# Two FFN channel blocks at a time: pair tiles in PSUM and instructions of 1024 columns

## The chip, the core and the metric

The kernel runs on one core of a Trainium2 chip. The metric is the device time of one execution in microseconds, the median of several runs. All runs told of here gave correct results. A ratio is the mean time of one kernel's fast runs over the mean of the other's fast runs of the same rounds, so it is not quite the ratio of the medians that stand beside it.

Engines are named as the profile names them: PE is TensorE, PEld its weight loads, DVE VectorE, ACT ScalarE, POOL GpSimd, SP the queue that issues DMAs.

## The reference, cut to what matters

An attention block with 32 inducing points is followed by a SwiGLU feed-forward block (FFN). B is 4, N 12416, C 128, and d_ff 1536, which is twelve channel blocks of 128.

```python
def mab(q, kv):                       # attention, softmax over the keys
    s = scale * (q @ kv.transpose(0, 2, 1))
    a = np.exp(s - s.max(-1, keepdims=True)); a /= a.sum(-1, keepdims=True) + 1e-09
    return a @ kv
x = mab(x, mab(I, x)).reshape(B * S, D)
xn = x / np.sqrt(np.mean(x * x, -1, keepdims=True) + 1e-06) * rms_g
g = xn @ w_gate
out = (g * (1 / (1 + np.exp(-g))) * (xn @ w_val)) @ w_out
```

## The kernel before

The FFN is done in 100 units of up to 512 tokens, each with twelve blocks. A *slot* is one block: a gate product, its silu on ACT, a value product, and the multiply of the two on DVE. The result `t` then has to be multiplied by `w_out` and summed over the blocks in `acc`. This *projection product* is not done at once. It goes into a queue, and each slot takes one or two products out of the queue between its gate and its value product. So PE has something to do while ACT and DVE work on the slot.

```python
for j in range(NJ):                                   # in ffn(), NJ = 12
    g = ps_gv.tile([P, 512], F32, name="gv", tag="gv")          # pool of 4 banks
    nc.tensor.matmul(g[:, 0:T], sg[:, ts(j, P)], a[:, 0:T], start=True, stop=True)
    sl = silp.tile([P, 512], F32, name="silu")
    nc.scalar.activation(sl[:, 0:T], g[:, 0:T], AF.Silu)
    products(j)                                       # takes products from the queue
    v = ps_gv.tile([P, 512], F32, name="gv", tag="gv")
    nc.tensor.matmul(v[:, 0:T], sv[:, ts(j, P)], a[:, 0:T], start=True, stop=True)
    t = up.tile([P, 512], F32, name="u")
    nc.vector.tensor_tensor(out=t[:, 0:T], in0=sl[:, 0:T], in1=v[:, 0:T], op=ALU.mult)
    steps(j)                                          # attention and seam work planned here
    if (b, u, j) in ready:
        soon(1, lambda j=j, t=t: three(j, t))         # a split: hi, lo, d
    else:
        plain.append(lambda j=j, t=t: project(wo[:, j, :], t[:, 0:T]))
```

A projection product is either *plain* (fp32) or *split*. In the split form `t` is taken apart into `hi`, `lo` and `d` by two ACT copies and two POOL subtractions, and three products on operands of type fp32r take the place of the fp32 one. In the trace an fp32r product of 512 columns takes PE 0.23 us and a plain fp32 one 0.86 us, so a split saves PE about 0.17 us. A loop plans the splits as far as POOL has time, and notes in `ready` from which slot on PE may use the operands. The queue is emptied like this:

```python
count = max(len(plain) - 1, 0) + sum(at <= now for at, _ in kara)   # kara: splits
... # held back for a few slots before an exponential
for _ in range(min(count, 2 if count > spare else 1)):   # spare is RESERVE = 3 mostly
    ...
# planning, per block:  (SLOT, SPLIT = 1.25, 2.75 us)
begin = max(free, now + 2.2 * SLOT)
...
free = begin + SPLIT
ready[b, u, j] = int((free + 0.3) / SLOT) + 1
```

Every four units there is a *seam*, where the attention weights of the next section are normed and prepared. Its last step, in slot 9 of a unit, is this:

```python
nc.vector.transpose(out=aT[rows, 0:w], in_=sc[b][rows, cols2[s]])
if b or s:
    nc.scalar.copy(out=hi[rows, 0:w], in_=aT[rows, 0:w])      # on ACT
...
engine.tensor_tensor(out=lo[...], in0=aT[...], in1=hi[...], op=ALU.subtract)   # on POOL
```

## Time and profile before

| | before |
|---|---|
| median of 3 runs | 1710.03 us (1707.98 to 1710.25) |
| span of the profiled run | 1708.1 us, mean granted PE clock 0.995 |
| silu, multiply | 1200 each, 0.60 and 0.68 us at 512 columns |
| plain products, splits | 817 and 383 |

The lines behind this are shown in the prediction. They are read in this order: the busy table says that only PE is full; the chain says that PE sets the end; the timeline of PE, start to start, says what a product costs.

Each stretch from one gate product to the next holds a known list of matmuls. The start-to-start steps of undisturbed stretches give each its time: 0.231 us for an fp32r product of 512 columns, 0.865 us for a plain fp32 one, less at 480 and 256 columns, and values found in the same way for the attention's products. What a stretch takes beyond the sum of its steps is called its *wait* here. From 90 us on, the waits of the kernel before sum to 61.9 us.

### The profile page before, as it was taken

Reading aid. Unit: us, or ns where it says so; the run is one execution under the profiler, and the core shown is the slowest. Engines: PE = TensorE matmul, PEld = TensorE weight load, DVE = VectorE, ACT = ScalarE, POOL = GpSimd, SP = SyncE. Lnnn points to the kernel's source line nnn. Section 1 sums busy time; section 2 is a strip of 40 time slices with the busy share of each in tenths; the row PEclk is TensorE's granted clock in tenths of the full one; section 3 lists DMA queues with packets and bytes.
Section 4 is the critical chain, followed back from the end, with each engine's and each line's share of the span. In section 5 each row is a group of like instructions: output and inputs, shape, how many; then the busy total and the mean of one; then the engine's idle time right before and its main releaser. Section 6 shows DMA issues by size and latency. Waiting matters only on the chain.

```text
span 1708.1 us, 23142 instructions
## 1 busy us (share of the span) xinstructions
PE 1668.0 (98%) x6781; PEld 1036.0 (61%) x6781; DVE 1145.0 (67%) x1914; ACT 1224.3 (72%) x2179; POOL 1146.2 (67%) x919
## 2 busy tenths in 40 slices
PE   8799999999999999999999999999999999999998
PEld 7445565655566666665556666566556666666666
DVE  4767775676667776667666777566756666666665
ACT  4446777676787777766678777767677887788786
POOL 1217775677587777677658777577657878887774
PEclk9899999999999999999999999999999999999999
DMA  6344533533354332433335314153211111111111
GB/s 261 74 68 75 70 80 60 121 75 69 56 78 68 49 65 51 105 75 88 65 57 90 57 34 87 28 131 79 54 31 33 35 36 33 33 36 36 33 37 24
DMA packets 389358, 112.64 MB, mean 66 GB/s; under 512 B 365136, under 2 KB 369776, under 8 KB 386672
## 3 DMA queue, kind: packets, MB, share of 16 engines
q1 hardware_dynamic: 388944, 111.02, 33.1%
q8 instruction: 54, 0.88, 0.2%
q14 instruction: 72, 0.59, 0.1%
q10 hardware_dynamic: 288, 0.15, 0.0%
HBM read 53.95 MB, written 27.00 MB: 47 GB/s over the span
## 4 chain that ended last, share of the span: by engine, by line
PE 87%; ACT 4%; DVE 3%; issue 2%; POOL 2%; DMA 1%; SPq 1%; ACTq 0%; DVEq 0%; POOLq 0%
PE acc L560 40%; PE gv L610 16%; PE gv L615 14%; PE u L578 5%; PE u L576 5%; PE mm L310 2%; DVE u L617 1%; PE mm L485 1%; ACT silu L612 1%; PE mm L368 1%; DVE aT L507 1%; PE gv L301 1%; ACT hi L510 1%; ACT hs L602 1%; POOL xn L603 1%
## 5 line engine op out<-in xcount | busy, mean ns | idle before, releaser
L617 DVE TENSOR_TENSOR u<-silu,gv 128x512 f32<-128x512 f32 (+2 forms) x1200 | 790.7, 666 | 512.1 <-PE gv L615 262.6
L612 ACT ACTIVATE silu<-gv 128x512 f32<-128x512 f32 (+2 forms) x1200 | 696.6, 584 | 370.1 <-PE gv L610 326.2
L560 PE MATMUL acc<-u,wo 128*128 128x512 f32 (+2 forms) x1634 | 811.5, 581 | 4.4 <-DVE u L617 3.1
L615 PE MATMUL gv<-a,sv 128*128 128x512 f32 (+2 forms) x1200 | 774.1, 645 | 3.7 <-DVE u L617 3.5
L598 POOL TENSOR_TENSOR xn<-u,xn 128x512 fp32r<-128x512 f32 (+2 forms) x383 | 482.2, 1259 | 356.0 <-ACT xn L597 295.1
L610 PE MATMUL gv<-a,sg 128*128 128x512 f32 (+2 forms) x1200 | 490.2, 409 | 12.8 <-ACT silu L612 8.5
L603 POOL TENSOR_TENSOR xn<-hs,u 128x512 fp32r<-128x512 f32 (+2 forms) x383 | 481.9, 1258 | 23.2 <-ACT hs L602 22.0
L610 PEld LDWEIGHTS gv<-a,sg 128*128 128x128 f32 x1200 | 227.2, 189 | 259.3 <-ACT silu L612 127.5
L560 PEld LDWEIGHTS acc<-u,wo 128*128 128x128 f32 x1634 | 305.1, 189 | 84.6 <-issue 18.2
L615 PEld LDWEIGHTS gv<-a,sv 128*128 128x128 f32 x1200 | 227.2, 189 | 204.1 <-issue 141.9
L597 ACT ACTIVATE xn<-u 128x512 fp32r<-128x512 f32 (+2 forms) x383 | 237.0, 619 | 15.6 <-DVE u L617 13.9
L602 ACT ACTIVATE hs<-xn 128x512 f32<-128x512 f32 (+2 forms) x383 | 235.7, 615 | 4.5 <-POOL xn L603 3.1
L560 PE MATMUL acc<-xn,xn 128*128 128x512 f32 (+2 forms) x383 | 149.7, 391 | 6.1 <-POOL xn L603 6.1
L578 PE MATMUL u<-xn,xn 128*128 128x512 f32 (+2 forms) x383 | 149.2, 390 | 0.0
L576 PE MATMUL u<-xn,xn 128*128 128x512 f32 (+2 forms) x383 | 147.8, 386 | 0.0
L499 POOL TENSOR_TENSOR rs<-ms,mhalf 128x16 f32<-128x16 f32 (+2 forms) x28 | 75.5, 2696 | 35.3 <-DVE ms L497 34.9
L560 PEld LDWEIGHTS acc<-xn,xn 128*128 128x128 f32 x383 | 71.8, 187 | 25.7 <-POOL xn L603 10.5
L578 PEld LDWEIGHTS u<-xn,xn 128*128 128x128 f32 x383 | 71.9, 188 | 15.6
L576 PEld LDWEIGHTS u<-xn,xn 128*128 128x128 f32 x383 | 72.1, 188 | 14.0
L569 DVE STREAM_TRANSPOSE o<-o 128x512 f32<-128x512 f32 (+2 forms) x97 | 67.7, 698 | 3.4
L568 DVE TENSOR_TENSOR o<-acc,o 128x512 f32<-128x512 f32 (+2 forms) x97 | 64.9, 669 | 0.0
L581 ACT ACTIVATE o<-u 128x512 f32<-128x512 f32 (+2 forms) x97 | 56.4, 581 | 0.2
(153 smaller groups left out, 735.0 us busy)
## 6 DMA issues: line engine op xcount, KB each, us to landing
out_dram<-o SPq DMA_DIRECT2D x320, 64.0 KB, 2.0
xT<-in_x_dram SPq DMA_DIRECT2D x60, 256.0 KB, 4.9
xn<-in_x_dram SPq DMA_DIRECT2D x60, 256.0 KB, 4.7
a<-hi SPq DMA_DIRECT2D x160, 64.0 KB, 2.0
a<-lo SPq DMA_DIRECT2D x158, 64.0 KB, 2.0
w<-w SPq DMA_DIRECT2D x22, 256.0 KB, 3.2
xn<-in_x_dram SPq DMA_DIRECT2D x5, 1024.0 KB, 10.9
out_dram<-o SPq DMA_DIRECT2D x64, 60.0 KB, 2.0
```

The source lines that it names most:

```text
L499: nc.gpsimd.tensor_tensor(out=rs, in0=ms, in1=mhalf[rows, 0:n], op=ALU.pow)
L560: nc.tensor.matmul(acc[:, 0:T], lhsT, rhs, start=st["left"] == NJ, stop=st["left"] == 1)
L576: nc.tensor.matmul(ups[:, 0:T], w[:, i, :], hi, start=st["k"] == nk, stop=False)
L578: nc.tensor.matmul(ups[:, 0:T], w[:, NK + i, :], lo, start=False, stop=not st["k"])
L597: nc.scalar.activation(hi, v, AF.Copy, scale=1.0 - 2.0 ** -13)
L598: nc.gpsimd.tensor_tensor(out=lo, in0=v, in1=hi.bitcast(F32), op=ALU.subtract)
L602: nc.scalar.activation(hs[:, 0:T], hi.bitcast(F32), AF.Copy, scale=1.0 + 2.0 ** -12)
L603: nc.gpsimd.tensor_tensor(out=d, in0=hs[:, 0:T], in1=v, op=ALU.subtract)
L610: nc.tensor.matmul(g[:, 0:T], sg[:, ts(j, P)], a[:, 0:T], start=True, stop=True)
L612: nc.scalar.activation(sl[:, 0:T], g[:, 0:T], AF.Silu)
L615: nc.tensor.matmul(v[:, 0:T], sv[:, ts(j, P)], a[:, 0:T], start=True, stop=True)
L617: nc.vector.tensor_tensor(out=t[:, 0:T], in0=sl[:, 0:T], in1=v[:, 0:T], op=ALU.mult)
```

## The change

The aim is fewer, larger elementwise instructions, so that fixed costs are paid half as often, and room for more splits. Blocks are taken in pairs; gate and value have one two-bank PSUM tile each; splits are made in pairs as well. To make room in SBUF, rows of x arrive in half tiles through one buffer, and the seam's product moves from POOL to DVE.

```diff
-    KJ = [j for j in range(NJ - 2) if j % 5 in (0, 2)] + [NJ - 3]
+    KJ = [j for j in range(NJ) if j % 4 < 2]
-    SLOT, SPLIT, RESERVE = 1.25, 2.75, 3
+    SLOT, UPPER, SPLIT, RESERVE = 1.25, 2.6, 4.85, 3
 ... (cut: pools, x rows in half tiles)
-        for j in range(NJ):
-            g = ps_gv.tile([P, 512], F32, name="gv", tag="gv")
 ... (cut: the loop shown above)
+        for j in range(0, NJ, 2):
+            pair = range(2)
+            g, v = (ps_gv.tile([P, 2, 512], F32, name=name) for name in ("g", "v"))   # bufs=1
+            for i in pair:
+                nc.tensor.matmul(g[:, i, 0:T], sg[:, ts(j + i, P)], a[:, 0:T], start=True, stop=True)
+            sl = silp.tile([P, 2, 512], F32, name="silu")
+            nc.scalar.activation(sl[:, :, 0:T], g[:, :, 0:T], AF.Silu)
+            products(j)
+            for i in pair:
+                nc.tensor.matmul(v[:, i, 0:T], sv[:, ts(j + i, P)], a[:, 0:T], start=True, stop=True)
 ... (cut: a slot of 1024 columns for u)
+            nc.vector.tensor_tensor(out=slot[0][:, :, 0:T], in0=sl[:, :, 0:T], in1=v[:, :, 0:T], op=ALU.mult)
+            steps(j)
+            products(j + 1)
+            steps(j + 1)
 ... (cut: three() on 1024 columns, with two sets of hi, lo, d in place of four)
-            nc.vector.transpose(out=z[...], in_=ps[rows, 0:w])
-            engine.tensor_tensor(out=z[...], in0=z[...], in1=weights(b, s), op=ALU.mult)
+            nc.vector.tensor_tensor(out=flat, in0=ps[rows, 0:w], in1=st["eT"][rows, 0:w], op=ALU.mult)
+            nc.vector.transpose(out=flat, in_=flat)
 ... (cut)
+            upper = now + 2 * SLOT + UPPER
+            begin = max(free, upper)
+            if begin > upper + SLOT:
+                continue
```

## The prediction

> **What bounds the kernel now.** I first read the busy table of the page, to see which engine has no room.
>
> ```profile
> span 1708.1 us, 23142 instructions
> PE 1668.0 (98%) x6781; PEld 1036.0 (61%) x6781; DVE 1145.0 (67%) x1914; ACT 1224.3 (72%) x2179; POOL 1146.2 (67%) x919
> PE 87%; ACT 4%; DVE 3%; issue 2%; POOL 2%; DMA 1%; SPq 1%; ACTq 0%; DVEq 0%; POOLq 0%
> ```
>
> The third line is the chain that ended last, by engine. TensorE is 98% busy and 87% of the chain; the other engines have 28 to 33% of the span free. Busy PE time is partly modelled, so I looked at how fast slots follow each other in the timeline of PE. A slot is one FFN channel block: gate product (L610), projection work, value product (L615).
>
> ```profile
> 805.30 0.39 PE L610 MATMUL gv<-a,sg 128*128 128x512 f32 x1
> 805.53 1.02 PE L560 MATMUL acc<-u,wo 128*128 128x512 f32 x2
> 805.99 0.79 PE L615 MATMUL gv<-a,sv 128*128 128x512 f32 x1
> 806.62 0.40 PE L610 MATMUL gv<-a,sg 128*128 128x512 f32 x1
> ...
> 813.32 0.39 PE L576 MATMUL u<-xn,xn 128*128 128x512 f32 x1
> 813.56 0.40 PE L578 MATMUL u<-xn,xn 128*128 128x512 f32 x1
> 813.79 0.39 PE L560 MATMUL acc<-xn,xn 128*128 128x512 f32 x1
> 814.02 0.40 PE L615 MATMUL gv<-a,sv 128*128 128x512 f32 x1
> 814.25 0.39 PE L610 MATMUL gv<-a,sg 128*128 128x512 f32 x1
> 814.49 0.59 PE L560 MATMUL acc<-u,wo 128*128 128x512 f32 x1
> ```
>
> Start to start, one fp32r product takes 0.23 us (813.56 to 813.79). A slot with the plain fp32 projection takes 806.62 - 805.30 = 1.32 us, so that projection costs 1.32 - 2 x 0.23 = 0.86 us. A slot whose projection is split into three fp32r products takes 5 x 0.233 = 1.165 us (813.32 to 814.49 is five such steps, 1.17). Over the whole trace the medians are 1.33 us (531 plain slots) and 1.16 us (251 split slots). So **one split saves PE about 0.167 us**. That is the only thing in this kernel that shortens PE's work, and the number of splits is limited by GpSimd and ScalarE, which make the three operands.
>
> I then subtracted these step times from all 1,199 intervals between gate products. About 40 us is left as waiting between 60 us, when the FFN starts, and 1700 us; some 10 us of it lies before 90 us, and some 10 us around the exponentials of the attention. So the rest of the run is PE work back to back.
>
> **The Trainium skill.** "FP8 and Floating Point Precision", section "TensorE Precision Notes", says that true fp32 takes four passes through the array. The trace agrees: 0.86 us is close to four times 0.23 us, and slightly less, so the split wins a little under one pass. "PSUM — Partial Sum Buffer", section "The four PSUM rules", says that one matmul's output fits in one bank; a 1024-column pair still needs two matmuls, so pairing removes no PE instruction. "Perfetto Trace Analysis", section "Optimizing Scalar/DVE Operations", says that each ScalarE and VectorE operation has a per-instruction overhead, that larger operations help an engine that is saturated, and that breaking them up can help where the engine isn't saturated but causes bubbles elsewhere. By the busy table the second case is nearer. The overhead shows in the groups kept apart by form:
>
> ```profile
> L617 DVE TENSOR_TENSOR u<-silu,gv 128x512 f32<-128x512 f32 x960 | 648.4, 682 | 409.0 <-PE gv L615 208.7 <-ACT hs L602 71.1 <-ACT xn L597 66.0
> L612 ACT ACTIVATE silu<-gv 128x512 f32<-128x512 f32 x960 | 570.6, 597 | 309.7 <-PE gv L610 269.2 <-DVE u L617 9.0 <-DVE xn L539 1.9
> L598 POOL TENSOR_TENSOR xn<-u,xn 128x512 fp32r<-128x512 f32 x318 | 410.2, 1290 | 272.5 <-ACT xn L597 219.8 <-PE gv L610 50.0 <-PE u L576 0.2
> L617 DVE TENSOR_TENSOR u<-silu,gv 128x256 f32<-128x256 f32 x48 | 19.4, 416 | 14.4 <-PE gv L610 5.5 <-PE gv L615 3.4 <-ACT silu L612 3.2
> L603 POOL TENSOR_TENSOR xn<-hs,u 128x256 fp32r<-128x256 f32 x15 | 11.0, 736 | 0.6 <-ACT hs L602 0.6
> L612 ACT ACTIVATE silu<-gv 128x256 f32<-128x256 f32 x48 | 18.2, 379 | 9.2 <-PE gv L610 9.0
> ```
>
> A straight line through 256 and 512 columns gives for 1024: DVE 682 + 2 x 266 = 1214 ns (fixed part 150), silu 597 + 2 x 218 = 1033 ns (161), POOL 1290 + 2 x 554 = 2398 ns (182). The two split copies on ACT (414 at 256, 627 to 631 at 512) become about 1055 ns. These are estimates from the trace.
>
> **The change part by part.**
>
> *Elementwise work.* 1200 silus become 600, about 604 us in place of 697; 1200 multiplies become 600, about 709 us in place of 791. Both engines run beside PE, so these 93 and 82 us are not on the path that sets the end. What they buy is room for splits.
>
> *More splits.* The planning loop at the end of the kernel is plain arithmetic. Worked through for the kernel before it gives 383, which is the x383 of the trace (318 of 512 columns, 50 of 480, 15 of 256). With the new constants (candidates are the pairs starting at 0, 4 and 8; 4.85 us of GpSimd a pair, which fits 2 x 2.398) it accepts 235 of 300 pairs: 9 fall at the ends, 21 at the marks for exponentials, 35 because GpSimd is planned busy. That is 470 splits (394, 64, 12), 87 more. Worth on PE: (76 x 0.167) + (14 x 0.157) - (3 x 0.08) = **14.6 us less**. PE matmul instructions rise by about 87 net, as a split has three and a plain product two.
>
> *Load after it.* POOL: 470 halves cost about 1105 us in place of 964, less 32 us for the product moved to DVE: some 1255 us. ACT: 1224 - 93 + 15 = about 1146. DVE: 1145 - 82 + 19 + 5 (product of the norm and extra partial sums) = about 1087. No engine reaches PE's total.
>
> *Buffers.* Before, gate and value products share four banks in turn, so a gate product waits for the silu of two slots earlier. After, gate and value have one two-bank tile each, and the next pair waits for the previous one. Take a pair with one plain and one split product, 4 x 0.2325 + 0.865 + 0.70 = 2.49 us on PE. Gate products start at 0 and 0.23, the second ends 0.40 later, silu runs from 0.66 to 1.69, and the bank pair is wanted at 2.49: slack 0.8 (0.6 in a pair with two splits, 2.33 us). The value products end near 1.9, the multiply runs to about 3.15, and they are wanted again at about 3.75: slack 0.6. In the kernel before the same sums give 1.3 to 1.5 us for both. A regular pair therefore does not stall, but PE has less reserve against a burst: the output step on DVE (683 + 712 ns), a seam transpose that ACT must wait for, or a hi or hs copy of 1.05 us. The trace before shows such a case near 820 us: DVE transposes aT until 819.77, ACT copies it until 820.40, silus follow, PE waits. With pairs I expect roughly 0.4 us more at each of the 24 seams and a few us elsewhere.
>
> *Moved work.* The norm's product goes from POOL to DVE (28 of 0.68 us), shortening that chain by 0.6 us each. Rows of x arrive in half tiles, five slots (6 us) ahead; landing takes 4.7 us at the median for twice the size, so I expect little waiting.
>
> *Sum.* -14.6 us of PE work, +5 to +9 us of waits: about -8 us, **1702 us**.
>
> **The rivals.** First: the single two-bank buffers stall PE in every pair. For it: slack falls from 1.4 to 0.6 us. Against it: it stays positive in the worst regular pair. A stall of 0.1 us in each of 600 pairs would be 60 us, and the time 1755. Second: nothing more stalls, or fewer handoffs even shorten the waits of 40 us by 5 to 10 us; the time is then 1686 to 1695. For it: half as many waits on ACT and DVE, and POOL loses a step in the seams; against it: the waits at start and exponentials do not depend on pairing. Third: GpSimd becomes the bound; a pair takes 4.80 us of POOL and two pairs take 4.98 us on PE, so a late operand stalls PE in order. The kernel before already has 7 such waits, 6.1 us. The planner keeps about 1 us in hand; if that fails at a tenth of 235 pairs by 1 us, it costs 23 us and the time is about 1720. Fourth: the x half tiles come late at some of the 36 uses; 0.5 us each is 18 us.
>
> **Range and chances.** Faster than 1676 needs over twice the gain of the splits, and waits cannot give back 20 us of 40: 0.04. Slower than 1744 needs a stall of the first rival's kind: 0.07. The rest, 0.89, is within 2%. Eight in ten: 1684 to 1727.
>
> **What would show it.** Right if the splits count 470, plain slots fall from 817 to 730, one 1024-column multiply takes near 1.21 us and the POOL steps near 2.4 us, the mean of a steady unit falls a little, and waits of PE on silu and multiply grow by less than 10 us. Wrong if pairs repeat slower than 2.49 us without POOL as releaser (first rival), or PE waits on L603's successor (third) or on x loads (fourth) by tens of us.

## The result

| | before | after |
|---|---|---|
| median | 1709.4 us (1707.98 to 1710.25, 4 runs) | 1786.39 us (1785.24 to 1787.85, 4 runs) |
| span, mean granted PE clock | 1708.1 us, 0.995 | 1785.1 us, 0.989 |
| plain products, splits | 817, 383 | 730, 470 |
| waits after 90 us, by the count above | 61.9 us | 152.4 us |

The ratio is 1.0452 (95% interval 1.0434 to 1.047): the changed kernel is 4.5% slower. These are the busy table and the chain of the changed kernel:

```profile
span 1785.1 us, 21312 instructions
PE 1684.9 (94%) x6868; PEld 1049.0 (59%) x6868; DVE 1122.3 (63%) x1360; ACT 1167.7 (65%) x1282; POOL 1259.7 (71%) x596
PE 73%; DVE 12%; issue 5%; ACT 4%; POOL 2%; DMA 2%; SPq 1%; DVEq 0%; ACTq 0%; POOLq 0%
```

PE is still the busiest engine, but its share of the chain has fallen from 87 to 73%, and that of DVE has risen from 3 to 12%. No engine is full. The groups kept apart by form show that each instruction costs what was foreseen (1214, 1033 and 2398 ns):

```profile
L645 ACT ACTIVATE silu<-g 128x1024 f32<-128x1024 f32 x480 | 491.8, 1025 | 328.6 <-PE g L643 258.0 <-DVE u L653 48.8 <-DVE xn L653 12.9
L653 DVE TENSOR_TENSOR u<-silu,v 128x1024 f32<-128x1024 f32 x386 | 469.9, 1217 | 388.1 <-PE v L648 318.2 <-ACT silu L645 59.3 <-POOL xn L629 7.3
...
L629 POOL TENSOR_TENSOR xn<-xn,u 128x1024 fp32r<-128x1024 f32 x158 | 379.2, 2400 | 9.3 <-ACT xn L628 7.0 <-DMA out_dram<-o 1.1
```

A regular pair runs as foreseen too. In the timeline of the changed kernel these are three gate pairs in a row, with one split and one plain product in each of the two pairs:

```profile
1502.96 0.63 PE L643 MATMUL g<-a,sg 128*128 128x512 f32 x2
...
1505.04 1.02 PE L643 MATMUL g<-a,sg 128*128 128x512 f32 x2
...
1507.92 0.39 PE L643 MATMUL g<-a,sg 128*128 128x512 f32 x1
```

Two pairs take 1507.92 - 1502.96 = 4.96 us, 2.48 us each; 2.49 had been worked out. (The middle start lies in the shadow of a plain product, as the records place the product after an fp32 pair some 0.4 us early.) Over the whole trace, 480 pairs hold two products; with that shadow taken out, half of them wait 0.02 us or less, but 85 wait over 0.25 us. So the time is lost in particular places. The list of waits has, of the kernel before (who waited for whom: us in total, times, longest):

```profile
ACT hi L510 <- DVE aT L507: 40.2, 27, 4.4
...
PEld gv L615 <- DVE u L617: 11.4, 27, 3.4
...
PE gv L610 <- ACT silu L612: 8.5, 16, 1.0
...
PE gv L615 <- DVE u L617: 3.5, 4, 3.0
```

and of the changed kernel:

```profile
PEld v L648 <- DVE u L653: 114.6, 268, 3.3
...
ACT hi L526 <- DVE aT L523: 47.7, 25, 4.6
...
PE g L643 <- ACT silu L645: 39.3, 36, 3.9
...
PE v L648 <- DVE u L653: 25.0, 41, 2.8
```

PE now waits for the silu (39.3 us, 8.5 before) and for the multiply (28.5 us, of which 3.5 us stand in a further line, where it was 3.5 before). ACT's own wait for the seam's transpose aT is hardly longer than before (40 and 48 us); in the kernel before it hardly reached PE.

One such place, in the timeline of the changed kernel (PE, DVE and ACT; start, duration, idle before):

```profile
490.20 0.65 DVE L587 TENSOR_TENSOR o<-acc,o 128x480 f32<-128x480 f32 x1
...
490.88 0.68 DVE L588 STREAM_TRANSPOSE o<-o 128x480 f32<-128x480 f32 x1
...
491.49 0.65 DVE L507 TENSOR_TENSOR z<-mm,eT 128x512 f32<-128x512 f32 x1
491.74 0.97 PE L643 MATMUL g<-a,sg 128*128 128x480 f32 x2
492.18 0.71 DVE L508 STREAM_TRANSPOSE z<-z 128x512 f32<-128x512 f32 x1
...
492.81 1.12 DVE L653 TENSOR_TENSOR u<-silu,v 128x960 f32<-128x960 f32 x1
493.85 0.41 DVE L523 STREAM_TRANSPOSE aT<-sc 32x256 f32<-32x256 f32 x1
493.98 0.70 PE L648 MATMUL v<-a,sv 128*128 128x480 f32 x2 [1.27 <-DVE u L653]
...
494.30 0.41 ACT L526 CAST hi<-aT 32x256 fp32r<-32x256 f32 x1 [2.11 <-DVE aT L523]
494.61 0.95 ACT L645 ACTIVATE silu<-g 128x960 f32<-128x960 f32 x1
...
495.62 0.83 PE L643 MATMUL g<-a,sg 128*128 128x480 f32 x2 [0.94 <-ACT silu L645]
```

Three things meet. No projection product stands between the gate products at 491.74 and the value products: the pair is *dry*. On DVE, the output step (o) and the seam's product and transpose (z) stand in front of the previous multiply, so the value tile is free late. And ACT stands idle for 2.11 us before the copy hi, until DVE has made aT, with the silu of this pair behind it. After two waits within four microseconds, PE runs slower for a while. The windows of this place (length, busy time and instructions of PE, PEld, DVE, ACT, POOL, then the granted PE clock, DMA share, GB/s) are:

```profile
491.50:495.00 3.50, 1.91 (x6) 0.68 (x4) 3.43 (x7) 1.39 (x3) 3.50 (x3) 1.00 0.36 56
495.00:498.00 3.00, 2.38 (x5) 1.35 (x6) 1.68 (x2) 2.91 (x4) 2.88 (x2) 0.67 0.71 113
498.00:501.50 3.50, 3.50 (x14) 2.68 (x12) 1.15 (x1) 1.38 (x2) 3.42 (x3) 0.79 0.41 72
```

The clock is granted in full, then at 0.67 and 0.79 on average. The Trainium skill's page "TensorE: Matmul & The Clock Gate", section "What's actually happening", says that the PE clock is halved after an idle window of about 3.4 us. The clock record agrees in the length: its dips are 3.4 us (or a multiple) at 0.5, but for the one at the very end. PE need not be idle all that time: in the 3.4 us before the dip at 496.0 us, PE was busy for 1.21 us. Half the length of the dips is 20.9 us after and 9.8 us before. That is the most that they can cost, as it counts PE's idle time in them and a tail past the last instruction; half of PE's busy time in them is 16.8 and 8.1 us. So 9 to 11 us of the loss of 77 us are such slow steps.

How often were pairs dry? In the trace after 90 us, 48 of 592 pairs hold no product or only one; they make up 63.8 of the 152.4 us of waits. In the kernel before, 28 of 1186 slots hold none, with 8.0 us. So 55.8 us of the 90.5 us by which the waits grew lie in dry pairs, and 34.7 us in the others. The reason is in the order in which instructions are issued: a pair split takes two products out of the queue for nine slots, where a single one took one out for five, and the reserve of three is soon used up. In the trace, 35 of the 48 are at block 10 of a unit, and 26 of these stand next to the seam's last step in slot 9. That the planning skips a pair there, as POOL is busy with the seam, was counted from the code.

### The profile page after: what moved, and what is told of

The parts are those of the page before. It is cut to its first block, busy times and chain, and to the rows that moved or that the text cites. A ratio compares the mean times of both kernels' runs of the same rounds, so it can differ in the third digit from the quotient of the medians.

```text
span 1785.1 us, 21312 instructions
## 1 busy us (share of the span) xinstructions
PE 1684.9 (94%) x6868; PEld 1049.0 (59%) x6868; DVE 1122.3 (63%) x1360; ACT 1167.7 (65%) x1282; POOL 1259.7 (71%) x596
## 4 chain that ended last, share of the span: by engine, by line
PE 73%; DVE 12%; issue 5%; ACT 4%; POOL 2%; DMA 2%; SPq 1%; DVEq 0%; ACTq 0%; POOLq 0%
PE acc L579 30%; PE v L648 13%; PE g L643 12%; DVE u L653 5%; PE u L595 5%; PE u L597 5%; PE mm L327 2%; ACT silu L645 2%; DMA xn<-in_x_dram 2%; PE mm L500 1%; DVE o L587 1%; POOL rs L515 1%; PE mm L384 1%; DVE xn L653 1%; DVE o L588 1%
## 5 line engine op out<-in xcount | busy, mean ns | idle before, releaser
L653 DVE TENSOR_TENSOR u<-silu,v 128x1024 f32<-128x1024 f32 (+2 forms) x482 | 572.9, 1189 | 495.0 <-PE v L648 405.2
L645 ACT ACTIVATE silu<-g 128x1024 f32<-128x1024 f32 (+1 forms) x600 | 599.3, 999 | 406.1 <-PE g L643 317.7
L621 POOL TENSOR_TENSOR xn<-u,xn 128x1024 fp32r<-128x1024 f32 (+1 forms) x191 | 445.5, 2333 | 242.0 <-ACT xn L620 171.0
L579 PE MATMUL acc<-u,wo 128*128 128x512 f32 (+2 forms) x1164 | 582.6, 585 | 3.0 <-POOL wo L280 2.8
L648 PE MATMUL v<-a,sv 128*128 128x512 f32 (+2 forms) x1200 | 507.9, 504 | 30.2 <-DVE u L653 25.0
L643 PE MATMUL g<-a,sg 128*128 128x512 f32 (+2 forms) x1200 | 494.7, 493 | 41.8 <-ACT silu L645 39.3
L629 POOL TENSOR_TENSOR xn<-xn,u 128x1024 fp32r<-128x1024 f32 (+1 forms) x191 | 447.3, 2342 | 12.0 <-ACT xn L628 9.5
L648 PEld LDWEIGHTS v<-a,sv 128*128 128x128 f32 x1200 | 219.7, 190 | 245.3 <-DVE u L653 114.6
L643 PEld LDWEIGHTS g<-a,sg 128*128 128x128 f32 x1200 | 218.7, 190 | 239.8 <-issue 140.4
L579 PEld LDWEIGHTS acc<-u,wo 128*128 128x128 f32 x1164 | 216.7, 189 | 75.7 <-issue 28.5
L628 ACT ACTIVATE xn<-xn 128x1024 f32<-128x1024 f32 (+2 forms) x235 | 242.9, 1034 | 0.0
L629 POOL TENSOR_TENSOR xn<-xn 128x1024 fp32r<-128x1024 f32 (+1 forms) x44 | 104.5, 2375 | 5.1 <-ACT xn L628 5.0
```

What stands on the lines that cost most here:

```text
L579: nc.tensor.matmul(acc[:, 0:T], lhsT, rhs, start=st["left"] == NJ, stop=st["left"] == 1)
L621: nc.gpsimd.tensor_tensor(out=lo[:, :, 0:T], in0=v, in1=hi[:, :, 0:T].bitcast(F32), op=ALU.subtract)
L628: nc.scalar.activation(hs, hi[:, :, 0:T].bitcast(F32), AF.Copy, scale=1.0 + 2.0 ** -12)
L629: nc.gpsimd.tensor_tensor(out=d[:, :, 0:T], in0=hs, in1=v, op=ALU.subtract)
L643: nc.tensor.matmul(g[:, i, 0:T], sg[:, ts(j + i, P)], a[:, 0:T], start=True, stop=True)
L645: nc.scalar.activation(sl[:, :, 0:T], g[:, :, 0:T], AF.Silu)
```

## The experiments

Names that begin with a_ start from the changed kernel, b_ from the kernel before; h_ is the changed kernel with the one-bank PSUM tiles put back. Each was timed in three rounds. All outputs are right. Medians in us; the kernel before was 1708 to 1710 in every set, so differences of 2 us between sets say nothing. Differences are read here from the 95% intervals, about 0.0015 to each side. The letters of the expectations are theories: D, pairs run dry; B, the single two-bank tiles stall any pair; M, the moved work; S, output step and seam meet on DVE; G, POOL is late; X, the silu waits behind the copy hi. The prediction had been that the splits alone are worth 14.6 us, so a kernel with 470 splits and the waits of before would take about 1695; that figure is an estimate and the yardstick below.

| run | us | ratio to before | waits after 90 us |
|---|---|---|---|
| changed kernel | 1786.4 | 1.0452 | 152.4 |
| a_res6 | 1758.6 | 1.0292 | 127.0 |
| h_halves | 1747.6 | 1.0227 | 116.3 |
| a_nosplit / b_nosplit | 1769.5 / 1764.1 | 1.0355 / 1.0321 | 57.6 / 52.5 |
| h_halves_res6, h_res6_tight | 1740.7, 1746.4 | 1.0183, 1.0224 | 109.5 (first) |
| a_seam_res6, a_kj04_res6 | 1746.3, 1754.2 | 1.0213, 1.0261 | 113.1, 102.1 |
| b_late4 | 1700.9 | 0.9949 | 53.4 |
| a_fin5, a_res6_fin5 | 1794.1, 1760.0 | 1.0503, 1.0307 | |
| b_newz | 1705.7 | 0.9986 | |
| a_hidve, a_seam | 1768.0, 1767.9 | 1.0347, 1.0346 | 133.9, 134.7 |
| h_hidve | 1721.9 | 1.0077 | 88.8 |
| p_late4 | 1734.2 | 1.0143 | 85.6 |
| a_res6_hidve | 1744.3 | 1.0202 | 111.3 |
| b_best | 1693.2 | 0.9908 | 49.3 |

### First set: dry pairs or buffers?

**a_res6**, more products kept back:

```diff
-    SLOT, UPPER, SPLIT, RESERVE = 1.25, 2.6, 4.85, 3
+    SLOT, UPPER, SPLIT, RESERVE = 1.25, 2.6, 4.85, 6
```

> The changed kernel with RESERVE 6 in place of 3, nothing else: products due are kept back up to six rather than drained to three. By counting the emission order this leaves 24 pairs with no or one projection product between their matmuls, where the changed kernel has 51. Theory D (the queue of projection products runs dry, and a dry pair cannot hide the silu and multiply of a single two-bank buffer; 1.7 us lost in each): 27 x 1.7 = 46 us less than the changed kernel's 1786, about 1740. Rival B (the single two-bank buffers stall PE in any pair, whatever lies between) and rival M (the moved work: half tiles of x, the norm's product on DVE): no change, 1780 to 1792.

It took 1758.6 us: 28 us less, not 46. So dry pairs matter, which B and M alone do not explain, but less than I had put down to them.

**h_halves**, the PSUM side undone:

```diff
-            g, v = (ps_gv.tile([P, 2, 512], F32, name=name) for name in ("g", "v"))
+            for i in pair:
+                g = ps_gv.tile([P, 512], F32, name="gv", tag="gv")      # pool of 4 banks
 ... (silu, v and multiply of 512 columns, into the halves of the same pair tiles)
```

> The changed kernel with the PSUM side undone: gate and value tiles of one bank from a rotation of four, silu and multiply of 512 columns, while the splits stay in pairs of 1024 columns, with the same plan (470 splits) and the same queue, so as many dry places. Theory D: a dry slot costs 0.28 us as in the kernel before, so the time falls by 70 to 90 us to 1697 to 1715. Rival B: the same, as the buffers are back. Rival M: stays near 1786, since none of the moved work is undone; each us above 1700 that is not seen in dry slots is M's.

It took 1747.6 us, 39 us less than the changed kernel, but 53 us over the yardstick. Both D and B had been expected to bring it under 1715: a miss. Something in the pair splits costs much even with the old buffers.

**a_nosplit** and **b_nosplit**, no splits in either:

```diff
-            if (j not in KJ or ...
+            if (True or j not in KJ or ...
```

> The changed kernel with no split at all: PE then has 470 x 0.165 = 78 us more work, ACT and POOL less. By counting, 17 pairs are dry instead of 51. Theory D: 1786 + 78 - 34 x 1.7 = about 1806, some 20 to 35 us over the kernel before without splits. Rival B: the stalls stay, about 1864, some 80 to 90 us over the kernel before without splits.

> The kernel before with no split at all, as the yardstick of the run without splits in pairs. One split saves PE 0.167 us, so 383 fewer cost 64 us: 1710 + 64 = 1774 by every theory; up to 10 us less if the splits caused waits too.

They took 1769.5 and 1764.1 us. The difference is 5 us, less than either theory had: without splits, the changed form costs next to nothing. And 470 splits, worth 78 us of PE work, make the changed kernel 17 us slower than none at all. 383 single splits gain the kernel before 55 of 64 us.

### Second set: lateness, and the place of the seam

**h_halves_res6** combines the two edits above.

> The run with one-bank tiles and pair splits (h_halves), with RESERVE 6 as well. By counting, slots without a projection product fall from 99 to 35. In h_halves such slots and the doubled ones after them lost some 64 us against 14 us in the kernel before. Theory D (dry queue): some 40 us less than its 1748, about 1707. If the dry slots were only where another wait showed itself, under 15 us less, over 1733.

1740.7 us, 7 us less than h_halves: a clear miss for D. Single dry slots cannot be what costs h_halves its 53 us. Its trace shows why little came of it: PE met POOL late instead (its list of waits has 16.0 us in 13 times for L629, against 6.3 in 6).

**a_seam_res6** moves the seam's last step in a_res6:

```diff
-                j = ((14, 17, 18, 21, 21, 33) if k else (32, 33, 33, 34, 34, 37))[i]
+                j = ((14, 17, 18, 21, 21, 28) if k else (32, 33, 33, 34, 34, 37))[i]
```

> The run with RESERVE 6 (a_res6), with the seam's last step (transpose aT, copies hi and lo) five slots earlier, in slot 4 of the unit in place of 9. Theory S (with splits due nine slots later, a unit's output step has moved from slot 4 to slot 9, where it meets the seam's transposes on DVE, and ACT waits for aT in front of a silu): 15 to 30 us less than 1759, 1729 to 1744. Without S: 1755 to 1760, as only three pairs more are split.

1746.3 us, 12 us less: the direction of S, short of its range.

**a_kj04_res6** leaves out the pairs at block 8:

```diff
-    KJ = [j for j in range(NJ) if j % 4 < 2]
+    KJ = [j for j in range(8) if j % 4 < 2]
```

> The run with RESERVE 6 (a_res6), with the pairs at 0 and 4 alone as candidates: 360 splits in place of 470, so 18 us more PE work; as many dry pairs (24 by counting). The last split of a unit is then due four slots earlier, so its output step leaves the seam's slots. Theory S: 20 to 35 us of waits go, so 1742 to 1757 in spite of the added work. Without S: 1777.

1754.2 us, in the range of S. But its trace shows the output step still in slot 9 (75 of 100 units), because six products kept back delay it as well. So it fits S for a reason that isn't S, and proves only that 110 splits fewer cost nothing here.

**b_late4** makes single splits late in the kernel before:

```diff
-            ready[b, u, j] = int((free + 0.3) / SLOT) + 1
+            ready[b, u, j] = int((free + 0.3) / SLOT) + 5
```

> The kernel before, its 383 splits untouched, but each taken up by PE four slots later than planned, so that a split takes nine slots as in the changed kernel. By counting, slots without a product rise from 36 to 64, and the output step moves to about slot 8. If lateness of the splits does harm by itself (D and S): 10 to 25 us more, 1719 to 1734. If it takes pairs to do harm: 1707 to 1712.

1700.9 us: *faster* by 0.5%, against my expectation. 56 slots are then dry in the trace, but 48 of them stand alone and wait 0.06 us each. Late operands are not harmful in themselves; the waits of PE for POOL, 6.1 us in 7 times before, are gone. They are not all of the gain of 9.3 us; the slow steps fell too (half of PE's busy time in the dips from 8.1 to 4.5 us). In h_halves, by contrast, 35 of the dry places are two slots in a row, with 1.03 us for the two.

### Third set: three more theories

**a_fin5** puts the output step off, **a_res6_fin5** does so with RESERVE 6:

```diff
-                soon(1, finish)
+                soon(6, finish)
```

> The changed kernel with the output step of each unit (sum and transpose on DVE) put off by five slots, nothing else: in its trace that step falls in slots 7 to 9, with the seam's product, transposes and sums (slots 9 to 11); five slots on it falls in slots 0 to 2 of the next unit. Theory S (collision of the two on DVE): in the trace 39 pairs that wait over 0.25 us and have both in them make up 57 us; I expect a third to a half of that back, 1757 to 1767. Theory D alone (dry pairs): the same dry pairs are left, 1783 to 1789.

> Both at once: RESERVE 6 and the output step put off by five slots. D and S together: a_res6 at 1759 less 20 to 35 us, 1724 to 1739. If S is nothing: 1759. If D and S are the same loss seen twice: no better than the better of the two alone.

1794.1 and 1760.0 us: 8 us more, and no change. S is wrong in the form "the output step meets the seam". In a_fin5's trace the output's transpose (o) stands within 2.5 us before only 10 of the 63 waits of PE over 0.25 us for a silu or a multiply, against 30 of 63 in the changed kernel; but the seam's transpose aT stands there in 30 of 63, against 31. The waits have stayed with the seam.

**h_res6_tight** splits only where POOL is free at once:

```diff
-            if begin > upper + SLOT:
+            if begin > upper + 0.1:
```

> The run with one-bank tiles, pair splits and RESERVE 6 (1741), whose trace has 13 waits of PE for GpSimd (some 21 us with the slow steps after them), with splits accepted only where GpSimd is planned free at once: by counting 422 splits in place of 470, which costs PE 8 us. Theory G (pair splits make GpSimd late, and a PE that doesn't run dry meets it): waits on GpSimd nearly vanish, 1717 to 1730. Otherwise: 1749.

1746.4 us where 1717 to 1730 was expected of G. But the edit missed its aim: waits of PE for L629 were to vanish nearly, and its trace has 21.1 us of them in 16 times, against 16.0 in 13 without it. So this run does not test G, and what POOL's lateness costs in this form stays open. In the changed kernel itself such waits are only 1.8 us.

**b_newz** gives the kernel before the change's two lines for z.

> The kernel before with the norm's product moved from GpSimd to DVE as in the change, nothing else. Theory M (the moved work is part of the loss): 5 to 15 us slower, 1715 to 1725. D and S: it stays in 1706 to 1713.

1705.7 us (ratio 0.9986, interval 0.9971 to 1.0001). The moved product does no harm. (No run undid the other moved work, the half tiles of x.)

### Fourth set: the chain through the seam's copy

Instead of guessing further I walked back from every wait of over 0.25 us: from the PE instruction to what released it, then to what that engine did before, or waited for. One chain stood out: silu on ACT, behind the copy hi on ACT, behind the transpose aT on DVE. It ends at waits of 43 us in the changed kernel, 36 in h_halves, 15 in a_nosplit, and 7 in the kernel before. (A recount from PE's idle gaps alone gives less, 36, 26, 9 and 2 us, in the same order.)

**a_hidve** and **h_hidve** take ACT out of it:

```diff
-            if b or s:
-                nc.scalar.copy(out=hi[rows, 0:w], in_=aT[rows, 0:w])
-            else:
-                nc.vector.tensor_copy(out=hi[rows, 0:w], in_=aT[rows, 0:w])
+            nc.vector.tensor_copy(out=hi[rows, 0:w], in_=aT[rows, 0:w])
```

> The changed kernel with the seam's copy hi on DVE in place of ACT, nothing else: ACT then never stands still in front of a silu until DVE has made aT; DVE has 27 copies of 0.7 us more. Theory X (the chain silu behind hi behind aT, at a pair that has run dry): the waits with that chain, 43 us, mostly go: 1746 to 1766. If the chain only shows a wait that would come anyway: above 1776.

> The run with one-bank tiles and pair splits (h_halves, 1748), with the same copy on DVE. Theory X: 20 to 36 us less, 1712 to 1728. Otherwise above 1740.

h_hidve took 1721.9 us, 26 us less than h_halves, within its range. a_hidve took 1768.0 us, 18 us less than the changed kernel, 2 us short of its range. The order of products is the same as without the edit, so the same pairs are dry: the 48 dry pairs of the changed kernel wait 63.8 us, those of a_hidve 28.1; the 90 dry slots of h_halves wait 48.8 us, those of h_hidve 17.5. A dry place costs much where this chain passes it, and less elsewhere: 0.2 us a slot are left in h_hidve, 0.6 us a pair in a_hidve. The lists of PE's waits of h_halves, h_hidve and a_hidve, in this order:

```profile
PE gv L644 <- ACT silu L645: 31.1, 33, 2.3
```

```profile
PE gv L641 <- ACT silu L642: 5.5, 10, 1.0
```

```profile
PE v L645 <- DVE u L650: 38.6, 59, 2.4
PE v L645 <- DVE xn L650: 7.5, 10, 2.0
PE g L640 <- ACT silu L642: 5.0, 14, 0.7
```

The wait for silu falls from 31.1 to 5.5 us in the one-bank form and from 39.3 to 5.0 us in the changed kernel. But with two-bank tiles, PE's wait for the multiply grows from 28.5 (25.0 + 3.5) to 46.1 us (38.6 + 7.5): the copy is now DVE work, and a late multiply holds the only value tile. With one-bank tiles it did not grow.

**a_seam** moves the seam's last step in the changed kernel, by the same edit as in a_seam_res6.

> The changed kernel (RESERVE 3) with the seam's last step in slot 4 in place of 9, away from the dry pairs at block 10. Theory X: 25 to 43 us less, 1743 to 1761, more than the 12 us that the same move gave with RESERVE 6, where most of those pairs were no longer dry. If dry pairs and seam add up independently: 12 us, about 1774.

1767.9 us, 18.5 us less; between the two ranges, so it does not tell them apart.

**b_best** is the kernel before with the late splits of b_late4, the copy on DVE, the z lines of b_newz, and no POOL time planned for them (403 splits in its trace):

> The kernel before with four things learnt: splits taken up four slots later (b_late4, 1701), the seam's copy hi on DVE, the norm's product on DVE, and no GpSimd time planned for it. In b_late4 the chain through hi still made up 13 us of waits. I expect 1688 to 1699, faster than both kernels.

1693.2 us, ratio 0.9908 (0.9894 to 0.9923): by the intervals faster than both kernels, and than b_late4. Its busy table:

```profile
span 1692.2 us, 23215 instructions
PE 1659.7 (98%) x6801; PEld 1040.7 (62%) x6801; DVE 1177.3 (70%) x1968; ACT 1229.7 (73%) x2192; POOL 1165.5 (69%) x932
```

It has more DVE and more ACT work than the changed kernel, and is 93 us faster.

### Fifth set: are the pair tiles enough?

**p_late4** puts the pair tiles alone on b_late4: two-bank gate and value tiles, silu and multiply of 1024 columns, splits still single, 383 of them. (To make room, the reciprocal is taken in place, and a small row shares a tile.)

```diff
-        for j in range(NJ):
-            g = ps_gv.tile([P, 512], F32, name="gv", tag="gv")
+        for j in range(0, NJ, 2):
+            g = ps_gv.tile([P, 2, 512], F32, name="g")      # bufs=1, v likewise
 ... (silu and multiply of 1024 columns; three() on each half)
```

> The kernel of b_late4 (single splits of 512 columns, 383 of them, 1701) with the pair tiles of the change alone: gate and value tiles of two banks, one each, silu and multiply of 1024 columns. (Two small tiles share space to make room.) If the two-bank tiles by themselves lose what lies between the changed kernel and h_halves: 1735 to 1745. If they lose it only in company of the pair splits, as without splits: 1703 to 1715.

1734.2 us, 33 us more than b_late4, with as many splits. It is at the edge of the first range: the pair tiles do harm without pair splits. That they do so only where there are splits is the difference from a_nosplit (5 us). Of the 33 us, 9 to 10 are slow steps (half the dips is 17.4 us against 7.4; half of PE's busy time in them 13.8 against 4.5). The run has one fault: ACT now waits 56.1 us in 145 times for the single buffer hs of the splits, against 4.9 in 13 in b_late4, which the changed kernel does not. In a recount some 5 of the 25 us of PE's idle gaps over 0.25 us lead back to that, and 19 to the copy hi.

**a_res6_hidve** has RESERVE 6 and the copy on DVE.

> The changed kernel with RESERVE 6 and the seam's copy hi on DVE. If the two add up: 1786 - 28 - 18 = 1740. If they cured the same waits (dry pairs at the seam): 1750 to 1758. What is then left over the 1695 that the splits alone would give is the single two-bank tiles meeting bursts on DVE.

1744.3 us: 42 us less than the changed kernel, where the sum of the two is 46. They add up nearly in full, so they cure mostly different waits. What is left over the yardstick is 49 us. The two-bank tiles cost 39 and 46 us in the other comparisons, but no run shows that they are these 49, as h_hidve is 27 us over the yardstick without them.

## Why the prediction was wrong

- **What bounds the kernel, and the value of a split: right.** The 470 splits came as counted. The PE work without waits fell from 1708.1 - 61.9 = 1646.2 to 1785.1 - 152.4 = 1632.7 us, by 13.5; 14.6 had been predicted.
- **Durations and load: right** within 1% for the three instructions, and within 10 us for POOL (1255 predicted, 1259.7), 22 us for ACT (1146, 1167.7) and 35 us for DVE (1087, 1122.3).
- **"A regular pair therefore does not stall": right for the usual pair,** 2.48 us against 2.49; 85 of the 480 pairs with two products did wait over 0.25 us.
- **The step that failed** is the term for waits: "I expect roughly 0.4 us more at each of the 24 seams and a few us elsewhere", in the sum "+5 to +9 us of waits". It was 90.5 us. (The parts do not make that sum either: 24 times 0.4 us is 9.6 us, before the few elsewhere.) The prediction's own sign shows the same step: waits of PE for silu and multiply were to grow by less than 10 us, and grew from 12.0 to 67.8 us. The mechanism that it names (less reserve against a burst, with the copy behind aT as the example) is the one that the runs show; the size was too small by a factor of ten, for three reasons. It took every pair to hold two products, while 48 pairs hold fewer and make up 55.8 us of the growth; whether the queue runs dry can be counted from the code, and I had not counted it. It took bursts one at a time, while output step, seam and copy meet in the same pair; taking the copy off ACT gives 18 us (a_hidve). And it left out that PE, after such waits, is clocked at half for 3.4 us: 9 to 11 us.
- **The first rival was dismissed on the regular pair alone.** Its form "in every pair" is indeed wrong, but its cost is real: putting the one-bank tiles back gives 39 us (h_halves), or 46 us with the copy on DVE (h_hidve against a_hidve), and adding pair tiles alone costs 33 us (p_late4, with the fault told there). Without splits they cost 5 us. Each of these edits changes three things together, the banks, the width of silu and multiply, and the order of the products between the matmuls; no run separates them. Why splits make the difference is argued, not shown: they put ACT copies of 0.6 to 1.05 us between the silus and shorten a slot on PE from 1.33 to 1.16 us, so the slack is smaller.
- **The other rivals: rightly set aside** for the changed kernel. PE's waits for POOL's operands were 1.8 us, for the halves of x 3.7 us. The moved product does nothing (b_newz).
- **Range and chances: wrong.** The time lies 59 us above the range, in an outcome that was given 0.07.

Taken apart in one order, from 1786 us: the two-bank tiles, with the wide instructions and the order that go with them, 39 (to 1748), the copy hi on ACT 26 (to 1722), and 27 us that remain over the yardstick of 1695. The trace of h_hidve has 88.8 us of waits against 61.9 before, the same 27; the walk finds there more waits for POOL and for halves of x and dry slots than before, but no run settled this remainder. The parts depend on the order: in the changed kernel the copy alone is worth 18 us and the larger reserve 28.

The page "Perfetto Trace Analysis" of the Trainium skill, section "Matmuls", says that independent matmul groups should rotate through different PSUM banks so that emptying one overlaps the matmuls of the next. Both kernels use the same four banks for it; with rotation by single banks PE waits for a slot two back, with pair tiles for the pair just before. The runs fit that sentence, with 33 to 46 us beside it where there are splits, though they do not test the banks alone. The sentence that the prediction cites from "Optimizing Scalar/DVE Operations" held in its second half: ACT and DVE were not saturated, and larger instructions saved 97 us of silu (696.6 to 599.3) and 80 us of multiply (790.7 to 711.2) on engines that had room, while they made bubbles on PE.

## What to carry to other kernels

When elementwise instructions are made larger at equal PSUM, the saving falls on engines that may not need it, and the slack of the busy engine shrinks; judge it where bursts meet and where the queue of filler work runs empty, not in the regular period. Count from the code how many periods have no filler before trusting the period. An in-order engine that waits for another in front of critical work (here a copy of 0.6 us) may be better given to the engine that it waits for, or moved. That, with later use of the split operands and the smaller edits of b_best, made the single-block kernel 0.9% faster; the copy alone was not tried there.

## What the Trainium skill lacked or had wrong

- "TensorE: Matmul & The Clock Gate", section "Why this matters for your kernels", advises no PE-idle gaps over about 3 us. Here the clock dipped to half for 3.4 us after two gaps of 1.27 and 0.94 us; PE was busy for 1.21 of the 3.4 us before the dip, and for 0.99 to 1.36 us before each of the five single dips after 200 us in the changed kernel. The same page, section "A second HAM failure mode: psum-queue depth-cycling", does tell of short idles between groups of matmuls that throttle the clock; it has no figure for how busy PE may be in a window that leads to a dip.
- "Perfetto Trace Analysis", section "Optimizing Scalar/DVE Operations", gives about 51 ns of overhead for ScalarE on PSUM, and says that profiled latency is about twice the busy overhead. The line through silus of 256 and 512 columns leaves 161 ns per instruction in the profile here, about three times 51, where twice 51 would be 102.
- No page says that late operands can pay: with splits used four slots later than planned (b_late4), the kernel before went from 1710.2 to 1700.9 us; PE's 6.1 us of waits for POOL are gone from its trace.
